# Reciprocal denominators of a linear-attention block spread over rows by a DRAM round trip instead of K=32 matmuls, with the order and the engines rearranged around it

## The chip, the cores and the metric

The kernel runs on one core of one Trainium2 chip. The metric is the device time of one execution in microseconds (us). Below, PE is TensorE (PEld its weight loads), DVE is VectorE, ACT is ScalarE, POOL is GpSimd and SP is SyncE, which issues the DMAs.

## The reference

An input `x` of 2048 tokens by 640 features is normalised; a linear attention with 32 heads of 20 features and a GELU MLP (640 to 1536 to 640) both work on the normalised input, and their results are added to `x`.

```python
def _A_ref(x, wqkv, wo):                       # x is the normalised input
    H = 32; Dh = D // H                        # 32 heads of 20
    q, k, v = ...                              # from x @ wqkv
    phi = lambda t: jnp.where(t > 0, t + 1, jnp.exp(t)) + 1e-6
    pq, pk = phi(q), phi(k)
    kv = jnp.einsum("bhsd,bhse->bhde", pk, v)
    z = jnp.einsum("bhsd->bhd", pk)            # sum of pk over the tokens
    num = jnp.einsum("bhqd,bhde->bhqe", pq, kv)
    den = jnp.einsum("bhqd,bhd->bhq", pq, z)[..., None] + 1e-6
    return (num / den, heads joined) @ wo
# out = x + _A_ref(xn) + (gelu(xn @ w1 + b1) @ w2 + b2)
```

## The kernel before

The tokens are treated in four groups of 512. For each group PE makes K, Q and `h` (the MLP's hidden layer). Then come `G` (the product of `xn` and `pk` over all tokens), `kv` (from `G` and the V weights), `KVW` (`kv` times `wo`) and sixteen output tiles, each the sum of an `h @ w2` part and a `pq @ KVW` part in one PSUM bank.

The attention's quotient needs one number per head and token, `1/den`, while `pqT` has one row per feature: each value must be copied to the 20 rows of its head. The kernel before lets PE do that, with a 0/1 matrix `Em4` of 32 rows (heads) as weights. DVE multiplies the result, in PSUM, into `pqT`:

```python
    lnden = ...                                      # room in hT[3], not yet in use
    nc.scalar.activation(out=lnden, in_=den[:], func=ACT.Ln, bias=tiny_t[:], scale=1.0)
    nc.scalar.activation(out=recT[:], in_=lnden, func=ACT.Exp, scale=-1.0)
    emit_G(2)

    def emit_pqs(c):
        rps = [bank() for _ in range(NG)]
        for i in range(NG):
            q = slice(i * H, (i + 1) * H)            # 32 rows: a quarter of the array
            nc.tensor.matmul(
                rps[i][:], lhsT=Em4[q, c * P : (c + 1) * P], rhs=recT[q, :], start=True, stop=True
            )
        for i in range(NG):
            gs = slice(i * TOK, (i + 1) * TOK)
            nc.vector.tensor_tensor(out=pqT[:, c, gs], in0=pqT[:, c, gs], in1=rps[i][:], op=ALU.mult)

    emit_pqs(0)
    emit_Ga(3)
    emit_pqs(1)
    emit_Gb(3)
    ...                                              # pqs(2) in G, pqs(3) and pqs(4) between h's of group 3
```

POOL keeps the running sum of `pk` (`zacc`, fifteen adds), builds masks, and adds `b2` to `x` (sixteen adds, late). For each of the first three groups a one-element copy on POOL, the gate, holds the group's sum back until DVE has normalised the last tokens of the group that follows (`[cut]` marks what is left out):

```python
            if j == 2 * TPG:
                nc.gpsimd.tensor_copy(out=Z3t[:, 0, 0:1], in_=xn[:, t1 + TPG - 1, 0:1])   # the gate
                emit_zacc(g)
    [cut]
    emit_emask()
    for t in range(NT):
        nc.gpsimd.tensor_tensor(out=x_all[:, t, :], in0=x_all[:, t, :], in1=b2b[:], op=ALU.add)
```

## Time and profile before

| | before |
|---|---|
| median of the first 5 runs | 215.76 us (215.42 to 215.78) |
| span of the profiled run | 213.9 us |
| PE busy | 208.9 us, 98% |
| DVE, ACT, POOL busy | 100.2, 83.6, 60.6 us |

First the page's line of busy times, then its line of the chain by engine (the chain of work that ended last, followed back from the end), then three groups of instructions (line, engine, operation, output <- inputs, shapes, count | busy us, mean ns | idle before, releaser):

```profile
PE 208.9 (98%) x1412; PEld 119.9 (56%) x1412; DVE 100.2 (47%) x249; ACT 83.6 (39%) x135; POOL 60.6 (28%) x82
PE 94%; DMA 2%; DVE 1%; SPq 1%; ACT 0%; issue 0%
...
L395 POOL TENSOR_TENSOR x_all<-x_all,b2b 128x640 bf16<-128x640 bf16 x16 | 21.7, 1385 | 0.0
L306 POOL TENSOR_TENSOR zacc<-zacc,pk 128x640 f32<-128x640 f32 x13 | 18.2, 1397 | 7.2 <-DVE pk L260 6.4
L457 DVE TENSOR_TENSOR pqT<-pqT,mm 128x512 bf16<-128x512 bf16 x20 | 12.3, 682 | 14.6 <-PE mm L452 14.6
```

PE is the chain, so an engine other than PE costs time only where PE has to wait for it. The busy share alone wouldn't say this: PE's ends are modelled, but the chain gives start-to-start times. Here are two parts of the chain of the kernel before, from within G and from KVW (start us, us, what):

```profile
107.80 0.89 PE mm L412 x16
108.69 0.33 PE mm L452 x4
109.02 3.56 PE mm L403 x16
112.58 0.33 PE mm L452 x4
112.90 1.00 PE mm L412 x16
113.90 3.45 PE mm L403 x16
...
128.40 0.54 PE mm L515 x4
128.94 0.25 PE mm L520 x4
129.19 0.65 PE mm L515 x4
129.84 0.25 PE mm L520 x4
130.09 0.38 PE mm L515 x2
130.47 0.37 PE mm L520 x2
130.84 1.19 PE mm L324 x5
```

L452 is the spreading by K=32 matmuls. Each group of four stands in the chain with 0.33 us, and the group behind it is 0.11 us longer than its clean twin (at L403 3.56 us at 109.02 against 3.45 at 113.90, at L412 1.00 us at 112.90 against 0.89 at 107.80). L515 and L520 are KVW: full-height matmuls, then some of 12 or 32 rows, three times over.

### The profile page before, as it was taken

What the parts mean: (1) busy time and instruction counts of PE and PEld (TensorE: products, weight loads), DVE (VectorE), ACT (ScalarE), POOL (GpSimd) and SP (SyncE); (2) the same over time, 40 slices, a digit from 0 to 9 for tenths busy, and PEclk for the clock granted to TensorE, in tenths of its full rate; (3) what the DMA queues carried; (4) which work ended last, traced back from release to release, by engine and by line L of the source; (5) the groups of instructions that cost most, each with busy time, mean ns of one, the idle gap of its engine ahead of it and who ended that gap; (6) DMA issues with size and microseconds to landing.
All of it is one profiled execution on the core that took longest, in us unless ns stands there. A gap on an engine that the chain in (4) does not pass through costs nothing.

```text
span 213.9 us, 3486 instructions
## 1 busy us (share of the span) xinstructions
PE 208.9 (98%) x1412; PEld 119.9 (56%) x1412; DVE 100.2 (47%) x249; ACT 83.6 (39%) x135; POOL 60.6 (28%) x82
## 2 busy tenths in 40 slices
PE   7899999999999999999999999999999999999994
PEld 2454455444554445545554563577777777777762
DVE  4689941999349970794044426622112112112111
ACT  3576769577885869741312736400000000000000
POOL 1000048910550018089899990000000000000000
PEclk9999999999999999999999999999999999999999
DMA  6999970000000000000000100000000110100011
GB/s 177 372 377 323 367 259 3 2 0 0 0 3 0 0 0 3 0 3 0 3 0 0 22 0 0 3 31 31 34 31 31 44 51 31 34 31 31 31 64 31
DMA packets 10079, 12.94 MB, mean 60 GB/s; under 512 B 2304, under 2 KB 8912, under 8 KB 10064
## 3 DMA queue, kind: packets, MB, share of 16 engines
q1 hardware_dynamic: 10064, 12.72, 17.6%
q8 instruction: 11, 0.18, 0.4%
q14 instruction: 4, 0.03, 0.0%
HBM read 10.10 MB, written 2.62 MB: 59 GB/s over the span
## 4 chain that ended last, share of the span: by engine, by line
PE 94%; DMA 2%; DVE 1%; SPq 1%; ACT 0%; issue 0%
PE mm L324 24%; PE mm L536 24%; PE mm L540 10%; PE mm L315 10%; PE mm L403 8%; PE mm L272 7%; DMA x_all<-in_A_x_dram 2%; PE mm L412 2%; PE mm L282 2%; PE mm L241 2%; PE mm L452 1%; PE mm L515 1%; PE mm L484 1%; PE mm L439 1%; DVE stats L196 0%; PE mm L520 0%
## 5 line engine op out<-in xcount | busy, mean ns | idle before, releaser
L536 PE MATMUL mm<-w,hT 128*128 128x320 bf16 (+2 forms) x384 | 57.4, 299 | 0.0
L324 PE MATMUL mm<-xnT,w 128*128 128x512 bf16 x240 | 54.1, 379 | 0.0
L536 PEld LDWEIGHTS <-hT 128*128 128x128 bf16 x384 | 37.2, 98 | 15.3
L544 DVE TENSOR_TENSOR late<-mm,x_all 128x320 bf16<-128x320 f32 (+2 forms) x32 | 15.7, 492 | 58.4 <-PE mm L540 58.4
L328 ACT ACTIVATE hT<-mm,b1col 128x512 bf16<-128x512 f32 x48 | 32.4, 686 | 16.0 <-PE mm L324 15.3
L324 PEld LDWEIGHTS <-w 128*128 128x128 bf16 x240 | 22.8, 98 | 26.6 <-issue 0.7
L256 ACT ACTIVATE e<-mm 128x512 bf16<-128x512 f32 x40 | 23.0, 596 | 12.3 <-PE mm L315 5.4
L540 PE MATMUL mm<-late,pqT 128*128 128x320 bf16 (+2 forms) x160 | 27.0, 299 | 0.0
L257 DVE TENSOR_SCALAR e<-e 128x512 bf16<-128x512 bf16 x40 | 15.0, 375 | 21.5 <-ACT e L256 21.4
L315 PE MATMUL mm<-xnT,wqk 128*128 128x512 bf16 x100 | 22.2, 379 | 0.0
L395 POOL TENSOR_TENSOR x_all<-x_all,b2b 128x640 bf16<-128x640 bf16 x16 | 21.7, 1385 | 0.0
L272 PE MATMUL mm<-wqk,xnT 128*128 128x512 bf16 x80 | 20.4, 379 | 0.7 <-DMA wqk<-in_A_wqkv_dram 0.7
L306 POOL TENSOR_TENSOR zacc<-zacc,pk 128x640 f32<-128x640 f32 x13 | 18.2, 1397 | 7.2 <-DVE pk L260 6.4
L457 DVE TENSOR_TENSOR pqT<-pqT,mm 128x512 bf16<-128x512 bf16 x20 | 12.3, 682 | 14.6 <-PE mm L452 14.6
L540 PEld LDWEIGHTS <-pqT 128*128 128x128 bf16 x160 | 15.5, 98 | 6.3
L403 PE MATMUL mm<-pk,xn 128*128 128x512 bf16 x80 | 18.1, 379 | 0.0
L378 POOL COPY Z3t<-xn 128x1 bf16<-128x1 bf16 x3 | 0.6, 186 | 57.8 <-DVE xn L232 57.8
L315 PEld LDWEIGHTS <-wqk 128*128 128x128 bf16 x100 | 9.6, 98 | 10.9
L196 DVE BATCH_NORM_STATS2 stats<-x_all 128x6 f32<-128x320 bf16 x32 | 13.6, 466 | 3.3 <-DMA x_all<-in_A_x_dram 3.3
L260 DVE SCALAR_TENSOR_TENSOR pk<-mm,e 128x512 bf16<-128x512 f32 x20 | 13.8, 692 | 1.0
L260 DVE SCALAR_TENSOR_TENSOR pqT<-mm,e 128x512 bf16<-128x512 f32 x20 | 13.8, 692 | 0.7
L403 PEld LDWEIGHTS <-xn 128*128 128x128 bf16 x80 | 7.5, 98 | 9.2 <-issue 0.7
(73 smaller groups left out, 132.4 us busy)
## 6 DMA issues: line engine op xcount, KB each, us to landing
w<-in_B_w_dram SPq DMA_DIRECT2D x2, 1920.0 KB, 10.0
out_dram<-late SPq DMA_DIRECT2D x15, 160.0 KB, 1.8
x_all<-in_A_x_dram SPq DMA_DIRECT2D x3, 640.0 KB, 11.9
wqk<-in_A_wqkv_dram SPq DMA_DIRECT2D x1, 800.0 KB, 7.3
wv<-in_A_wqkv_dram SPq DMA_DIRECT2D x1, 800.0 KB
woA<-in_A_wo_dram SPq DMA_DIRECT2D x5, 160.0 KB, 8.7
wqk<-in_A_wqkv_dram SPq DMA_DIRECT2D x1, 480.0 KB, 4.9
x_all<-in_A_x_dram SPq DMA_DIRECT2D x2, 160.0 KB, 2.3
```

The lines of the kernel that those rows point to most:

```text
L256: nc.scalar.activation(out=e[:], in_=ps[:], func=ACT.Exp)
L260: nc.vector.scalar_tensor_tensor(out=dst, in0=shaped(ps), scalar=0.0, in1=shaped(e), op0=ALU.max, op1=ALU.add)
L272: nc.tensor.matmul(K_ps[t][:], lhsT=xnT[:, k, t * P : (t + 1) * P], rhs=wqk[:, k, D : D + TOK], start=(k == 0), stop=(k == NC - 1),)
L306: nc.gpsimd.tensor_tensor(out=zsum if u == NT - 1 else zacc[:], in0=pk[:, 0, :] if u == 1 else zacc[:], in1=pk[:, u, :], op=ALU.add,)
L315: nc.tensor.matmul(ps[:], lhsT=wqk[:, k, m * P : (m + 1) * P], rhs=xnT[:, k, gs], start=(k == 0), stop=(k == NC - 1),)
L324: nc.tensor.matmul(ps[:], lhsT=w1[:, k, j * P : (j + 1) * P], rhs=xnT[:, k, g * TOK : (g + 1) * TOK], start=(k == 0), stop=(k == NC - 1),)
L328: nc.scalar.activation(out=hT[g][:, j, :], in_=ps[:], func=ACT.Gelu_apprx_tanh, bias=b1col[:, j : j + 1], scale=1.0)
L395: nc.gpsimd.tensor_tensor(out=x_all[:, t, :], in0=x_all[:, t, :], in1=b2b[:], op=ALU.add)
L403: nc.tensor.matmul(ps[:], lhsT=w, rhs=pk[:, t, 0:TOK], start=(t == 0), stop=(t == NT - 1))
L536: nc.tensor.matmul(ps, lhsT=hT[g][:, j, i * P : (i + 1) * P], rhs=w2[:, j, ns], start=(j == 0), stop=False)
L540: nc.tensor.matmul(ps, lhsT=pqT[:, c, t * P : (t + 1) * P], rhs=KVW[:, c, ns], start=False, stop=(c == NC - 1),)
L544: nc.vector.tensor_tensor(out=osb[:, ns], in0=ps, in1=x_all[:, t, ns], op=ALU.add)
```

## The change

It wants the K=32 matmuls off PE. `recT` is written to DRAM, each row twenty times, and read back as a matrix of full height; DVE multiplies it into `pqT` from SBUF. The rows land in `xnT`, so everything that reads `xnT` must be done: `h` of group 3 moves ahead of G. `zacc` and `x + b2` move from POOL to DVE, `1/den` is DVE's reciprocal instead of Ln and Exp on ACT, KVW is made in two groups instead of three with parts of the first two output tiles between them, and PSUM banks are handed out by an explicit rotation. The core of the diff:

```diff
+    rec_rows = dram.tile([NG * H * DH, TOK], BF16, name="rec_rows")
-    def bank(dtype=F32):
-        return psum.tile([P, TOK if dtype == F32 else 2 * TOK], dtype, name="mm", tag="mm")
+    def bank(dtype=F32, hold=False):
+        n = turn.pop(0)
+        (held if hold else turn).append(n)
+        return psum.tile(... name=f"bank{n}", tag=f"bank{n}")
 [cut]
+    def emit_den():
+        [cut: the same twenty matmuls]
+        nc.vector.tensor_scalar(out=zacc[:, 0:TOK], in0=den[:], scalar1=1e-6, scalar2=None, op0=ALU.add)
+        nc.vector.reciprocal(out=recT[:], in_=zacc[:, 0:TOK])
+        nc.sync.dma_start(
+            out=rec_rows[:].rearrange("(q r) s -> q r s", r=DH),
+            in_=recT[:].unsqueeze(1).to_broadcast((P, DH, TOK)),
+        )
+    def emit_xb(t):
+        nc.vector.tensor_tensor(out=x_all[:, t, :], in0=x_all[:, t, :], in1=b2b[:], op=ALU.add)
 [cut: emit_zacc from nc.gpsimd to nc.vector]
-        for j in range(NJ if g < NG - 1 else 0):
+        for j in range(NJ):
             emit_h(g, j)
+            if g == 1 and j == 2 * TPG:
+                emit_zacc(0)
+                emit_zacc(1)
+            if g == 2 and j == 2 * TPG:
+                gate(xn[:, NT - 1, 0:1])
+                emit_masks()
+                emit_zacc(2)
+            if g == 3 and j == 0:
+                emit_zacc(3)
+            if g == 3 and j == 4:
+                emit_z()          # and half of the x + b2 adds
+            if g == 3 and j == 5:
+                emit_den()        # and the other half
 [cut]
-    emit_pqs(0)
-    emit_Ga(3)
-    [cut]
+    emit_Ga(0)
     for c in range(NC):
+        nc.sync.dma_start(out=xnT[:, c, :].rearrange("p (i s) -> p i s", i=NG),
+            in_=rec_rows[:].rearrange("(i d) s -> d i s", i=NG)[c * P : (c + 1) * P, :, :])
+        nc.vector.tensor_tensor(out=pqT[:, c, :], in0=pqT[:, c, :], in1=xnT[:, c, :], op=ALU.mult)
 [cut]
+    emit_hw(0, halves[0], hold=True)     # the h @ w2 part of an output tile
+    emit_KVW(halves[0])                  # five banks, full-height first, then the rest
+    emit_hw(0, halves[1], hold=True)
+    emit_KVW(halves[1])
```

## The prediction

> **What bounds it now.** The page of busy times gives TensorE (PE) 208.9 of 213.9 us; VectorE (DVE) 47%, GpSimd 28%. The chain of waits is 94% PE, and after 8.3 us it shows no PE wait: matmuls stream back to back (1.08 us per five 128x512, 1.63 us per twelve 128x320) at a granted clock of 1.0. So only PE time removed, or a new PE stall, can move the total.
>
> **What the change removes from PE.** The twenty K=32 matmuls that spread the reciprocal denominators over rows. In the chain each of the five groups is 0.33 us, and the group behind it is longer than its clean twin: 3.56 against 3.45, 1.00 against 0.89 (twice), 1.19 against 1.08, 3.34 against 3.24, about 0.11 us each. The Trainium skill (TensorEngine Tiling, Key Properties) says that changing the tiling mode drains TensorE; this trace agrees, at about 0.1 us a switch. Together 5 x 0.44 = 2.2 us, all critical. The KVW product goes from three alternations of full and 12/32-row matmuls (2.44 us plus 0.11 behind) to two: estimate 0.2 us less. Sum: -2.4 us.
>
> **What it adds, off PE.**
> - Running sum zacc: from GpSimd (1.40 us each, 15 of them) to DVE. Estimate from a PSUM-source 512-element op at 0.69 us: 0.8 us each for 640 fp32 elements. Seven in group 1 (54.8 to about 60.2 us; the next phi needs DVE near 61.2) and four in group 2 fit in idle DVE time. The last four follow the last phi (about 96.2 us without the GpSimd contention that stretches the 0.28 us clamp to 0.83) and end near 99.4; PE wants zsum at 99.6. Tight: 0 to 0.4 us of stall.
> - x+b2 on DVE: the Trainium skill (VectorE: DVE Perf Modes, the perf-mode tier table) gives a bf16 SBUF tensor_tensor 2x, 1224 ns at 2048 elements; estimate 0.45 us for 640, 16 of them, in idle time.
> - Reciprocal on DVE replaces Ln and Exp. Its cost I don't know: 0.7 to 4.3 us.
> - A DRAM round trip: 2.6 MB written and read in 1 KB rows. The page has 12.72 MB in 17.6% of the span, so about 60 ns per 1.26 KB packet and engine; estimate 8 us plus 2 us landing each way. den ends near 102 us, recT near 105 to 109, written by 119, last product pqT by 127 to 131. DVE then needs kv at about 132.6 and PE needs pqT at about 141. It fits by 2 to 5 us; if not, kv's eviction waits in DVE order behind the pqT products, and PE stalls before KVW.
>
> **Prediction.** 213.5 us (-1.1%), 212.7 to 214.8 in 8 of 10 cases. Faster by over 2%: 0.03; within 2%: 0.92; slower by over 2%: 0.05.
>
> **What would show it.** Right: no K=32 recT matmuls in PE's timeline; G and h groups at 3.45, 0.89 and 1.08; DVE busy up about 12 us, GpSimd down 40 us; output tiles still 2.31 us; about 5 MB more DMA between 105 and 130 us; PE waits under 0.5 us in total. Wrong: a PE wait on zsum near 100 us, on Z3t before den, or on kv near 134 us.
>
> **What would make it wrong.** A DRAM round trip above 25 us, or a slow reciprocal on top of it, stalls PE before KVW by microseconds; DVE falling behind in the K stages, so that PE waits for PSUM; a larger stall at zsum.

## The result, and the profile after

| | before | after |
|---|---|---|
| median | 215.66 us (215.34 to 215.78, 13 runs) | 213.51 us (213.47 to 213.93, 7 runs) |
| ratio to before | | 0.9908 (0.9898 to 0.9918) |
| PE busy in the profiled run | 208.9 us | 207.0 us |
| DVE, POOL busy | 100.2, 60.6 us | 112.5, 13.2 us |

A ratio here is the mean time of one kernel's runs over that of the other's of the same rounds, so it isn't quite the ratio of the medians quoted. Executions over 1.5% slower than the fastest of the same kernel are left out of the means.

The page's busy line and the groups that answer to those of before:

```profile
PE 207.0 (98%) x1392; PEld 119.9 (56%) x1392; DVE 112.5 (53%) x265; ACT 82.7 (39%) x134; POOL 13.2 (6%) x41
...
L473 DVE TENSOR_TENSOR pqT<-pqT,xnT 128x2048 bf16<-128x2048 bf16 x5 | 6.1, 1225 | 13.1 <-DMA xnT<-rec_rows 13.1
L337 DVE TENSOR_TENSOR zacc<-zacc,pk 128x640 f32<-128x640 f32 x13 | 10.8, 828 | 0.4
```

The chain of the changed kernel, from the start of G:

```profile
108.88 3.45 PE bank L446 x16
112.33 0.89 PE bank L455 x16
...
132.67 1.74 PE bank L526 x12
134.41 0.68 PE bank L545 x5
135.09 0.37 PE bank L549 x5
135.46 1.74 PE bank L526 x12
137.20 0.68 PE bank L545 x5
137.88 0.37 PE bank L549 x5
138.25 3.37 PE bank L526 x24
```

G is clean: all five groups are 3.45 and 0.89 us. KVW (L545, L549) is 2 x (0.68 + 0.37) = 2.10 us in place of 2.44, and 0.11 us longer for each of the two groups behind it (1.74 against 1.63 us for twelve 128x320 matmuls, and 3.37 against 3.26 for 24).

DVE's timeline shows the new chain beside PE's (start, us, engine, line, operation, count, [idle before <- releaser]):

```profile
98.85 0.83 DVE L337 TENSOR_TENSOR GT<-zacc,pk 128x640 bf16<-128x640 f32 x1
...
104.29 3.35 DVE L326 RECIPROCAL recT<-zacc 128x512 bf16<-128x512 f32 x1
...
128.79 1.23 DVE L473 TENSOR_TENSOR pqT<-pqT,xnT 128x2048 bf16<-128x2048 bf16 x1 [1.64 <-DMA xnT<-rec_rows]
131.84 0.69 DVE L512 TENSOR_TENSOR late<-bank,zacc 128x512 bf16<-128x512 f32 x1 [1.82 <-PE bank L495]
```

The sum is ready 0.2 us before PE takes it at 99.87 us, and the last product ends 1.8 us before DVE takes `kv` (L512). PE waits for nothing after its first stage: the view of PE's waits has only 0.9 us for the first K weights and the 1.1 us at the very start.

### A ruler that leaves out the noise

The span of a profiled run splits into three parts (the timed figure is longer than the span by 1.7 to 2.0 us, in `e1_pe_spread` by 2.3 to 2.5): up to the first Q matmul, from there to the start of DVE's last add, and the rest. The first part depends on how the first loads land (13.63 to 14.39 us in the fourteen profiled kernels, whose code is nearly the same up to there). The last part is the last stores and SP's final waits. The middle part is where the change is. I call it the stretch; in the table the median and ratio come from the timed runs, the other columns from the one profiled run. Three kernels in which PE has the same work and no wait after its first stage (after, `e7_trip_plus8`, `e12_gpsimd_gated`) agree within 0.03 us in the stretch.

| kernel | median us | ratio to before (95%) | first Q at | stretch | rest |
|---|---|---|---|---|---|
| before | 215.66 | | 14.14 | 197.00 | 2.8 |
| after | 213.51 | 0.9908 (0.9898 to 0.9918) | 14.39 | 194.64 | 3.2 |
| e1_pe_spread | 215.89 | 1.0015 (1.0003 to 1.0028) | 13.91 | 196.92 | 2.7 |
| e4_k32_five | 215.81 | 1.0002 (0.9989 to 1.0015) | 13.63 | 196.80 | 3.2 |
| e5_k32_block | 215.09 | 0.9973 (0.9960 to 0.9985) | 14.04 | 196.15 | 3.2 |
| e6_k128_five | 214.71 | 0.9947 (0.9934 to 0.9961) | 14.05 | 195.71 | 3.2 |
| e10_kvw_three | 213.56 | 0.9909 (0.9895 to 0.9922) | 13.81 | 194.86 | 3.2 |
| e3_gpsimd_adds | 214.07 | 0.9937 (0.9923 to 0.9950) | 13.65 | 195.22 | 3.2 |
| e12_gpsimd_gated | 213.56 | 0.9899 (0.9887 to 0.9912) | 14.29 | 194.61 | 3.2 |
| e2_dma_alone | 224.01 | 1.0397 (1.0380 to 1.0414) | 13.99 | 204.75 | 3.4 |
| e11_dma_and_adds | 214.41 | 0.9937 (0.9925 to 0.9949) | 14.14 | 194.83 | 3.7 |
| e7_trip_plus8 | 213.10 | 0.9886 (0.9869 to 0.9904) | 13.79 | 194.63 | 2.8 |
| e8_trip_plus20 | 217.99 | 1.0129 (1.0090 to 1.0169) | 13.91 | 199.31 | 2.8 |
| e9_trip_plus20_kv_first | 215.12 | 0.9978 (0.9957 to 0.9999) | 13.82 | 196.96 | 2.8 |

The change takes 197.00 - 194.64 = 2.36 us out of the stretch.

### The profile page after: what moved, and what is told of

Read it like the earlier page. It is cut to its first block, busy times and chain, and to the rows that moved or that the text cites. A ratio compares the mean times of both kernels' runs of the same rounds, so it can differ in the third digit from the quotient of the medians.

```text
span 212.2 us, 3414 instructions
## 1 busy us (share of the span) xinstructions
PE 207.0 (98%) x1392; PEld 119.9 (56%) x1392; DVE 112.5 (53%) x265; ACT 82.7 (39%) x134; POOL 13.2 (6%) x41
## 4 chain that ended last, share of the span: by engine, by line
PE 94%; DMA 3%; DVE 1%; SPq 1%; ACT 0%; issue 0%
PE bank L526 25%; PE bank L355 24%; PE bank L534 10%; PE bank L346 10%; PE bank L446 8%; PE bank L269 7%; DMA x_all<-in_A_x_dram 3%; PE bank L455 2%; PE bank L279 2%; PE bank L238 2%; PE bank L495 1%; PE bank L545 1%; PE bank L318 1%; DVE stats L193 0%; SPq L117 0%; PE bank L549 0%
## 5 line engine op out<-in xcount | busy, mean ns | idle before, releaser
L526 PE MATMUL bank<-w,hT 128*128 128x320 bf16 (+2 forms) x384 | 57.2, 299 | 0.0
L355 PE MATMUL bank<-xnT,w 128*128 128x512 bf16 x240 | 53.8, 379 | 0.0
L538 DVE TENSOR_TENSOR late<-bank,x_all 128x320 bf16<-128x320 f32 (+2 forms) x32 | 15.7, 492 | 54.5 <-PE bank L534 54.5
L359 ACT ACTIVATE hT<-bank,b1col 128x512 bf16<-128x512 f32 x48 | 32.5, 686 | 14.1 <-PE bank L355 13.2
L253 ACT ACTIVATE e<-bank 128x512 bf16<-128x512 f32 x40 | 23.0, 596 | 11.8 <-PE bank L346 7.1
L534 PE MATMUL bank<-late,pqT 128*128 128x320 bf16 (+2 forms) x160 | 26.5, 299 | 0.0
L346 PE MATMUL bank<-xnT,wqk 128*128 128x512 bf16 x100 | 22.2, 379 | 0.0
L269 PE MATMUL bank<-wqk,xnT 128*128 128x512 bf16 x80 | 20.4, 379 | 0.9 <-DMA wqk<-in_A_wqkv_dram 0.9
L254 DVE TENSOR_SCALAR e<-e 128x512 bf16<-128x512 bf16 x40 | 11.4, 285 | 13.6 <-ACT e L253 13.6
L446 PE MATMUL bank<-pk,xn 128*128 128x512 bf16 x80 | 18.1, 379 | 0.0
L257 DVE SCALAR_TENSOR_TENSOR pk<-bank,e 128x512 bf16<-128x512 f32 x20 | 13.8, 692 | 1.0
L473 DVE TENSOR_TENSOR pqT<-pqT,xnT 128x2048 bf16<-128x2048 bf16 x5 | 6.1, 1225 | 13.1 <-DMA xnT<-rec_rows 13.1
```

The lines of the kernel that those rows point to most:

```text
L253: nc.scalar.activation(out=e[:], in_=ps[:], func=ACT.Exp)
L254: nc.vector.tensor_scalar(out=e[:], in0=e[:], scalar1=1.0, scalar2=1e-6, op0=ALU.min, op1=ALU.add)
L257: nc.vector.scalar_tensor_tensor(out=dst, in0=shaped(ps), scalar=0.0, in1=shaped(e), op0=ALU.max, op1=ALU.add)
L269: nc.tensor.matmul(K_ps[t][:], lhsT=xnT[:, k, t * P : (t + 1) * P], rhs=wqk[:, k, D : D + TOK], start=(k == 0), stop=(k == NC - 1),)
L346: nc.tensor.matmul(ps[:], lhsT=wqk[:, k, m * P : (m + 1) * P], rhs=xnT[:, k, gs], start=(k == 0), stop=(k == NC - 1),)
L355: nc.tensor.matmul(ps[:], lhsT=w1[:, k, j * P : (j + 1) * P], rhs=xnT[:, k, g * TOK : (g + 1) * TOK], start=(k == 0), stop=(k == NC - 1),)
```

## The experiments

My theory: the gain is the PE time of the K=32 groups, streaming plus a change of tiling mode on either side (2.2 us), and one KVW alternation less (0.2 us); all else is hidden. Rivals: the gain comes from the new order, the bank rotation or the work taken off POOL; or the K=32 groups cost only their streaming. Then there was a question of what the hidden part can bear.

### Putting the spreading back on PE

`e1_pe_spread` is the changed kernel without the DRAM trip and with `Em4` and `emit_pqs` of before, one call behind each G group (the last one inside it):

```diff
-        nc.sync.dma_start(out=rec_rows..., in_=recT...)
-    for c in range(NC):
-        [cut: read rec_rows into xnT, multiply]
     emit_Gb(0)
-    for j in range(1, NC):
-        emit_G(j)
+    emit_pqs(0)
+    for j in range(1, NC - 1):
+        emit_G(j)
+        emit_pqs(j)
+    emit_Ga(NC - 1)
+    emit_pqs(NC - 1)
+    emit_Gb(NC - 1)
```

> The changed kernel, with only the spreading of the reciprocals put back on TensorE (five groups of four K=32 matmuls inside G); everything else of the change stays. If those matmuls were the gain: TensorE's chain grows by 5 x 0.44 = 2.2 us, ratio to the kernel before 0.999 (215.4 to 215.8 us), and G groups of 3.56 or 1.00 come back behind them. Rival, the gain came from the new order, the bank bookkeeping or the work moved off GpSimd: it stays near 213.5 us, ratio 0.991. In between would mean that both play a part.

Measured: 215.89 us, the stretch 2.28 us longer than the changed kernel's. The order, the banks, the adds on DVE and the two KVW groups are all still there, and nearly nothing is left of the gain. The rival falls. The timed ratio, 1.0015, is a little above the expected 0.999. The stretch, 196.92 against 197.00 us, doesn't show that excess. The record places it outside the profiled span: the spans of its five runs are 213.5 to 213.6 us, no longer than those of the kernel before in the same rounds (213.4 to 213.9), but the time is 2.28 to 2.51 us longer than the span there, against 1.86 to 1.97. What takes it is open. Of the 2.28 us, 2.17 lie inside G (23.90 us of chain from its start to `kv` against 21.73).

### What a K=32 group costs

Three kernels add dummy matmuls to the changed kernel's G; nobody reads their results.

```diff
+    def emit_k32(n):
+        for _ in range(n):
+            pd = [bank() for _ in range(NG)]
+            for i in range(NG):
+                q = slice(i * H, (i + 1) * H)
+                nc.tensor.matmul(pd[i][:], lhsT=identity[q, :], rhs=recT[q, :], start=True, stop=True)
+    def emit_k128(n):
+        for _ in range(n):
+            nc.tensor.matmul(bank()[:], lhsT=identity[:], rhs=recT[:], start=True, stop=True)
 # e4: emit_k32(1) in five places; e5: emit_k32(5) in one; e6: emit_k128(1) in five places
```

> The changed kernel with twenty K=32 dummy matmuls of 512 columns, four at a time in five places of G; nothing reads their results and the output stays right. Theory, stream plus switch: 5 x 0.44 = 2.2 us more, ratio 0.999, 215.7 us. Rival, only the columns that stream cost (four run side by side, 0.216 us a group): 1.1 us more, 214.6 us.

> The same twenty K=32 dummy matmuls in one block behind three groups of G. Theory: one pair of switches instead of five, 5 x 0.22 + 0.22 = 1.3 us more, 214.8 us, 0.9 us less than in five places. Rival, the cost goes by the matmul and not by the switch: the same 2.2 us as in five places.

> The changed kernel with one full K=128 dummy matmul of 512 columns in each of the five places: as many streamed columns as a group of four K=32 side by side, and no change of tiling mode. Theory: 5 x 0.216 = 1.1 us more, 214.6 us, half of what the K=32 groups cost. Rival, any insertion between accumulation groups costs 0.44 us: 2.2 us.

Measured in the stretch: +2.16 us in five places, +1.51 us in one block, +1.07 us with full-height matmuls. The chain of the first one, then of the second, then of the third:

```profile
112.46 0.33 PE bank L481 x4
112.79 3.56 PE bank L446 x16
```

```profile
121.56 1.42 PE bank L481 x20
122.98 3.56 PE bank L446 x16
```

```profile
112.88 0.22 PE bank L485
113.09 3.45 PE bank L446 x16
```

A full-height matmul of the same 512 columns costs 0.22 us and leaves its neighbour alone. A group of four K=32 matmuls costs 0.33 us and lengthens its neighbour by 0.11 us. So in five places about half of the 2.16 us is streaming (1.07 us) and half goes with entering and leaving the mode. The Trainium skill (TensorEngine Tiling, Key Properties) says that a change of tiling mode drains TensorE; here a change costs 0.11 us each way. In the trace of the first kernel the first weight load after a change starts only after a pause of about 0.1 us, where in the third it runs ahead of its matmul. No run separates the drain from the load that can't run ahead.

The block came out 0.2 us above my 1.3, and the records of its single matmuls show why: the twenty start in six steps of about 0.216 us (4, 3, 4, 3, 4 and 2 at a time), not in five. One of the eight banks is held by G, so the eighth matmul writes the bank of the first again; from the eighth on each waits for a semaphore that PE's own matmuls raise. Six steps and one pair of changes are 6 x 0.216 + 0.22 = 1.52 us, against 1.51 measured. The extra 0.2 us is thus of the dummies' making, and a further group costs its streaming alone.

### Two or three KVW groups

```diff
     emit_hw(0, halves[0], hold=True)
-    emit_KVW(halves[0])
+    emit_KVW([(m, halves[0]) for m in range(NG)])
+    emit_KVW([(NC - 1, halves[0]), (NC - 1, halves[1])])
     emit_hw(0, halves[1], hold=True)
-    emit_KVW(halves[1])
+    emit_KVW([(m, halves[1]) for m in range(NG)])
```

> The changed kernel with the KVW product in three alternations of full and row-tiled matmuls, as before the change, in place of two. If each alternation costs a switch: the chain's KVW part grows by 0.2 to 0.3 us, ratio 0.9918, 213.7 us. Rival, the number of alternations doesn't matter: unchanged, 213.5 us.

Measured: the stretch is 0.22 us longer, as expected. The timed ratio (0.9909 against 0.9908) doesn't resolve it: its interval is 0.27% wide, or 0.6 us. What a chain shows to 0.02 us can't be had from five rounds of times.

### The DRAM trip alone, in the old order

`e2_dma_alone` is the kernel before, with nothing changed but the spreading. The rows land in places that are dead by then: the first three token groups of `xnT`, and rows 7 to 11 of the last `hT`.

```diff
+    nc.sync.dma_start(out=rec_rows..., in_=recT broadcast...)      # behind the Exp
     def emit_pqs(c):
-        [cut: four matmuls, four products from PSUM]
+        for ss, rec in ((slice(0, S - TOK), xnT[:, c, 0 : S - TOK]), (slice(S - TOK, S), hT[NG - 1][:, NJ - NC + c, :])):
+            nc.vector.tensor_tensor(out=pqT[:, c, ss], in0=pqT[:, c, ss], in1=rec, op=ALU.mult)
```

> The kernel before, with only the spreading replaced by the DRAM round trip (Ln and Exp stay on ScalarE, adds stay on GpSimd, h of group 3 stays behind G; the rows land in dead parts of xnT and hT3). If the K=32 matmuls were the gain: 213.6 us, ratio 0.990, about 0.2 us above the full change for the three KVW groups, provided the products end before the output tiles at about 136 us. Rival: without the new order the round trip isn't hidden, and the time is 215 us or more.

It took 224.01 us, 8.5 us more than the kernel before in the same rounds (215.53 us). Both theories missed: my own by the time, and the rival by the reason, since the trip itself was punctual (the first rows were there at 118.4 us). DVE's timeline, then POOL's, then PE's wait:

```profile
118.42 10.50 DVE L454 TENSOR_TENSOR pqT<-pqT,xnT 128x1536 bf16<-128x1536 bf16 x1 [19.47 <-DMA xnT<-rec_rows]
...
129.18 0.95 DVE L454 TENSOR_TENSOR pqT<-pqT,xnT 128x1536 bf16<-128x1536 bf16 x1
```

```profile
106.44 21.66 POOL L386 TENSOR_TENSOR x_all<-x_all,b2b 128x640 bf16<-128x640 bf16 x16
```

```profile
PE mm L513 <- DVE late L497: 5.4, 1, 5.4
```

The first product took 10.50 us, its twin of the next chunk 0.95. It ended at 128.92 us, 0.8 us after POOL's row of sixteen adds (106.44 + 21.66 = 128.10 us): it ran when they were through. The Trainium skill (SBUF — State Buffer, Terms) describes a pair of SBUF ports shared by DVE and GpSimd: exclusive, held for a whole instruction, and "the loser fully blocks". This trace agrees, and goes further: DVE lost not one instruction of POOL's but about seven in a row ((128.10 - 118.42) / 1.354, from 21.66 us for sixteen). The kernel before never met this: one operand of its products lay in PSUM, and they took 682 ns each while the same adds ran.

To test that reading, `e11_dma_and_adds` moves only the sixteen adds to DVE as well:

```diff
-    for t in range(NT):
-        nc.gpsimd.tensor_tensor(out=x_all[:, t, :], in0=x_all[:, t, :], in1=b2b[:], op=ALU.add)
 [cut]
+    for t in range(NT):       # behind the product of gmask and z
+        nc.vector.tensor_tensor(out=x_all[:, t, :], in0=x_all[:, t, :], in1=b2b[:], op=ALU.add)
```

> The kernel before with the spreading by DRAM, as in the run that did that alone, and with the sixteen x+b2 adds moved from GpSimd to VectorE, ahead of the products. In the run without that move the first product took 10.5 us instead of 0.95 and ended when GpSimd's row of adds ended. Theory, the adds on GpSimd kept the two-SBUF-input product off the SBUF: now the products take 0.95 and 0.41 us, kv is evicted near 123 us as soon as it is there, no TensorE wait before KVW, 213.6 us, ratio 0.990; from the first Q matmul to the last VectorE add 194.8 us. Rival, the order of before can't hide the round trip, whoever adds: a wait before KVW of microseconds stays, 218 us or more.

```profile
118.47 0.96 DVE L454 TENSOR_TENSOR pqT<-pqT,xnT 128x1536 bf16<-128x1536 bf16 x1 [10.90 <-PE mm L315]
```

The product takes 0.96 us, PE doesn't wait before KVW, and the stretch is 194.83 us, the 194.8 expected: all of the change's gain but the 0.2 us of KVW. The time, 214.41 us, is above the 213.6 expected, by what the last part of the run takes (3.7 us against 2.8 before; see below). So of all that the change rearranges, two things carry the gain in the stretch: the spreading off PE, and the x+b2 adds off POOL so that a product with both inputs in SBUF can run. The new order was not needed for it.

### The adds back on POOL

```diff
         for u in range(max(1, g * TPG), (g + 1) * TPG):
-            nc.vector.tensor_tensor(
+            nc.gpsimd.tensor_tensor(        # and the same in emit_xb
```

> The changed kernel with the fifteen running sums and the sixteen x+b2 adds back on GpSimd. If only TensorE's chain counts: 213.5 us, ratio 0.990 to 0.992, although VectorE's busy time falls by about 18 us and its clamp is slowed again; masks for kv end near 129 us, just before they are needed at 132. Rival, the relief of VectorE from GpSimd contention was part of the gain: 214 us or more.

Measured: 214.07 us and 0.58 us more in the stretch, so not "the same". The chain of this run, in group 1:

```profile
42.23 0.78 DVE e L254
43.04 0.69 DVE pqT L257
43.73 0.77 DVE e L254
...
54.68 0.46 DVE xn L229
55.18 0.45 PE bank L238 x5
```

The clamps (L254, the minimum with 1 inside `phi`) take 0.77 us where others in the same chain take 0.21; the slow ones are those beside which POOL sums group 1 (41.46 to 47.29 us); DVE falls behind until the normalisation `xn` is late and PE's transposes (L238) start late. But my undo was not a clean one: the kernel before has a gate on the sums of groups 0, 1 and 2, and the change had dropped the first two, which on DVE aren't needed. `e12_gpsimd_gated` puts them back:

```diff
-            if g == 1 and j == 2 * TPG:
-                emit_zacc(0)
-                emit_zacc(1)
-            [cut]
+            if g < NG - 1 and j == 2 * TPG:
+                gate(xn[:, t1 + TPG - 1, 0:1])
+                emit_zacc(g)
+                if g == 0:
+                    emit_masks()
```

> The changed kernel with its adds back on GpSimd as in the run before, but each group's sum held back until that group's last normalisation, as the kernel before the change holds it. That run lost 0.6 us in group 1, where the ungated sums stretched VectorE's clamps from 0.21 to 0.77 us until the normalisation was late. Theory, it was the moment and not the engine: from the first Q matmul to the last VectorE add 194.6 to 194.8 us (195.2 in that run), time 213.5 us, ratio 0.991. Rival, work on GpSimd costs wherever it stands: 195.2 us again, 214.1 us.

Stretch 194.61 us, time 213.56 us: the 0.6 us is gone. In this order the engine of the adds doesn't matter, only the moment. Here the x+b2 adds on POOL end at 119.3 us, just before the first product starts (119.95 us). The five products then run beside a row of twenty mask selects on POOL and still take only 1.23 to 1.38 us each. So not every row on POOL holds such a product back to its end; why the row of adds did in `e2_dma_alone` isn't shown.

### How much longer the trip may take

Extra rows, written to a spare DRAM tensor ahead of the real ones, delay the trip; the third kernel also puts DVE's eviction of `kv` ahead of the products.

```diff
+        nc.sync.dma_start(out=spare[:, 0:8, :], in_=recT[:].unsqueeze(1).to_broadcast((P, 8, TOK)))
         nc.sync.dma_start(out=rec_rows..., in_=recT...)          # e7: 8 rows; e8 and e9: 20
```

> The changed kernel with 1.05 MB written to a spare DRAM tensor ahead of the reciprocals' rows, on the same queue: the round trip gets longer by 1.05/0.36 = about 3 us. The trace of the change shows the last product end at 130.0 us, 1.8 us before VectorE takes kv, and kv evicted 1.9 us before TensorE needs it: 3.7 us of slack. Expected: products end near 133, a TensorE wait of 0 to 0.3 us, 213.5 us. Rival, no slack, the trip is on the chain: 3 us more, 216.5 us.

> The same with 2.6 MB written ahead: the trip is longer by about 7.3 us, 3.6 us more than the slack. Expected: TensorE waits about 3.6 us before KVW, for kv, whose eviction stands behind the products in VectorE's order: 217.1 us (216 to 218). Rival, the slack is that of the products themselves, wanted only at 141.6 us: no wait, 213.5 us.

> The same 2.6 MB ahead, with the eviction of kv put before the five products in VectorE's order. If it is the order that stalls TensorE, the wait before KVW goes; the products end near 137.5 us, before the 141.6 us where TensorE wants them, but KVW's evictions stand behind the products now. Expected: 213.5 to 214.5 us. Rival, something else of the longer trip costs (DMA traffic, the landing itself): 217 us as before.

With 8 rows the reads are issued 2.2 us later (119.30 against 117.11 us); the stretch is unchanged, 194.63 us. With 20 rows they are issued at 124.74 us, the last product ends at 136.14 instead of 130.02 us, and PE waits (PE's timeline, then stretches of 4 us with busy time and counts of PE, PEld, DVE, ACT, POOL, then the granted clock, DMA share and GB/s):

```profile
136.79 0.85 PE L550 MATMUL bank<-woA,late 128*128 128x320 bf16 x5 [2.89 <-DVE late L517]
...
138.17 3.22 PE L531 MATMUL bank<-w,hT 128*128 128x320 bf16 x12
```

```profile
134.00:138.00 4.00, 1.21 (x10) 0.52 (x10) 2.80 (x5) 0.00 (x0) 0.00 (x0) 0.96 0.08 23
138.00:142.00 4.00, 4.00 (x19) 2.15 (x19) 0.89 (x2) 1.08 (x3) 0.00 (x0) 0.61 0.02 4
```

The wait is 2.89 us (3.6 expected), so the slack was about 136.14 - 130.02 - 2.89 = 3.2 us, near my 3.7. But the stretch grew by 4.67 us: after the wait the granted clock fell to a mean of 0.61 for 4 us (in finer stretches 0.50 from 137.7 to 141.1 us), and twelve matmuls took 3.2 us instead of 1.7. The same shows in `e2_dma_alone`, where the clock was 0.50 from 132 to 140 us after the wait of 5.4 us. In these two runs the wait cost its own length and then some slow matmuls.

With `kv` first the wait for `kv` goes and the clock stays at 1.00, but the time is 215.12 us instead of the 213.5 to 214.5 expected. PE's waits say what took its place:

```profile
PE bank L551 <- DVE late L559: 0.7, 1, 0.7
PE bank L555 <- DMA late<-in_A_wo_dram: 0.7, 1, 0.7
```

KVW's evictions (L559) stand behind the five products now, and the last pieces of `wo`, on the same queue behind the reads, come late; the five matmuls that need them take 1.01 us instead of 0.44. These three make 2.0 of the 2.32 us by which the stretch is longer than the changed kernel's. So the order on DVE made the stall of the run before, and what is left of the delay came out at the next two places.

### The part after the last add

The kernel with 8 extra rows is the fastest of all by the median, 213.10 us, although it does more and its stretch equals the changed kernel's. Its rest is 2.8 us against 3.2. The records of SP's last instructions in the trace show SP going through five final waits and then a drain. The drain starts 0.19 us after the last store has landed in the kernel before, 0.55 us after in the changed one (a pause of 0.44 us stands between its last wait and its drain), and 0.28 us after with the extra rows. There the pauses come before the landing, or overlap it. The whole wind-down from the last landing takes 0.94, 1.43 and 1.05 us, and 1.93 us in `e11_dma_and_adds`. The kernel with the spreading back on PE, whose DMAs are those of before, has 0.94 us again. What the pause is, I didn't settle, and the difference of 0.4 us in the medians lies within the two intervals of the ratios.

## Why the prediction was right

- **The sum.** 213.5 us was predicted, 213.51 measured. The prediction counted 2.4 us off PE; the stretch lost 2.36.
- **The K=32 groups.** 5 x 0.44 = 2.2 us was predicted; putting them back costs 2.28 us, dummies in their place 2.16. Half of it is streaming and half is changing modes; counting streamed columns alone would have given 1.1.
- **KVW.** 0.2 us was predicted; undoing it alone costs 0.22.
- **Stall at zsum.** 0 to 0.4 us was predicted. The sum ended at 99.68 us (predicted 99.4), PE took it at 99.87, and there was no wait. An add took 0.83 us (0.8 estimated).
- **The trip.** recT was predicted for 105 to 109 us and came at 107.6; the write landed 9.3 us after its issue (10 predicted); the last product ended at 130.0 us (127 to 131). The reciprocal took 3.35 us, inside the wide 0.7 to 4.3. The slack, predicted as 2 to 5 us, came out at about 3.2.
- **Busy times.** DVE rose by 12.3 us (12 predicted). POOL fell by 47.4 us and not 40: I had left out the 6.7 us of masks for `Em4` that go too.
- **What the prediction didn't have.** SP's end is 0.5 us longer after the change, and the first stage varies by 0.8 us between kernels. That the median fell onto the predicted value to 0.01 us is therefore partly luck. The prediction also didn't see that POOL must be through with x+b2 when the products start; it listed the move to DVE as a cost only. In the old order the move was a condition for the gain; in the new one the same adds on POOL end in time (`e12_gpsimd_gated`). The 8.5 us loss of the trip without that move shows how near a miss lay.

## What to carry to other kernels

Where one engine is the whole chain, price a change by that engine's start-to-start times in the chain, including the longer neighbour of a group in another tiling mode, and check the rest only for "is it there in time, with how much slack". Before a VectorE operation gets its second operand from SBUF instead of PSUM, look at what GpSimd runs at that moment: a row of its two-input adds can hold the operation back until the row ends. And when an undo doesn't give the old time back, compare the gates and waits that the change dropped before believing in an effect.

## What the Trainium skill lacked or had wrong

- SBUF — State Buffer (Terms): the shared port pair is said to be held for a full instruction. Here VectorE lost it for about seven GpSimd adds in a row, 10.50 us for an operation of 0.95. Nothing is said of a whole row of instructions. It isn't so for every row: in `e12_gpsimd_gated` the same kind of product took 1.23 to 1.38 us beside a row of twenty GpSimd selects.
- TensorE: Matmul & The Clock Gate (Part 1): the clock is said to fall after at least one idle window of about 3.4 us. Here a recorded wait of 2.89 us, to 136.79 us, was enough: the granted clock was 0.50 from 137.7 to 141.1 us.
- TensorEngine Tiling (Key Properties): the drain at a change of mode has no figure. Here a change between full-height and K=32 matmuls took 0.11 us each way.
- VectorE: DVE Perf Modes: no time for the reciprocal. Here 128x512 fp32 to bf16 took 3.35 us. Its 1224 ns for a two-input bf16 operation of 2048 elements held: 1225 ns.
- No page has the program's own wind-down from the landing of its last store to the end of its span, which took 0.94 to 1.93 us in programs with the same last stores.
